# Ninety-six stores of a weight conversion, begun by GpSimd instead of SyncE

## The chip, the cores and the metric

The kernel runs on one core of a Trainium2 chip. The time is device microseconds of one execution, from the first to the last instruction on that core and what lies around them. The engines of the core have queues of their own and work through them in order: TensorE (PE in the profile, with its weight loads as PEld), VectorE (DVE), ScalarE (ACT), GpSimd (POOL) and SyncE (SP), which here only begins transfers. Sixteen DMA engines carry the transfers of all of them.

## The reference

Attention with the heads mixed before and after the softmax, followed by a two-layer feed-forward net. All of it is float32.

```python
# q, k, v: (8, 12, 448, 64); w_pre, w_post: (12, 12)
scores = (1 / 8) * q @ k^T                          # per batch and head
scores = einsum('bhij,hg->bgij', scores, w_pre)     # mix the heads
attn = exp(scores - max) ; attn /= sum(attn) + 1e-9
attn = einsum('bhij,hg->bgij', attn, w_post)        # mix the heads again
x = (attn @ v), heads side by side: (3584, 768)
h = x @ w_in                                        # (768, 2048)
out = (h - tanh(h)) @ w_out                         # (2048, 768)
```

## The kernel before, in words

The program has two stages. The first, up to about 850 us, is attention; the second is the feed-forward net. The second stage multiplies in a split form (a high and a low part of each number) and takes seven products where eight are usual, so it needs the weights of `w_in` and `w_out` as high and low parts, and sums of their quarters in the same form. These are made once, during the first stage, by the class `Convert` and its generator `narrow_quad`, and written to tensors in the chip's DRAM: `wi` and `wo` hold the split weights, `ss` and `ts` the split sums. The second stage loads them from there.

**Attention.** 448 query rows of each of 8 batches are cut into blocks of 120, 120, 120 and 88 rows, and these into groups of at most ten rows times twelve heads. Two groups make a *place*; there are 180 places (`NPL`), and the loop over `p` writes one place after another. In place `p`:

- SP begins the gathers of a later place: `gather` (L907) copies the scores of ten rows and twelve heads from the tile `s` into one of six tiles `t`, 210 KB each, for place `p + 2`.
- SP then begins up to six other transfers that were put into two lists, `queue` (loads of q, k, v, stores of `x`) and `slow` (all transfers of the conversion); `send`, L766, is the line that begins each.
- PE mixes the heads of place `p` (`premix`, L918, tile `ps_p`). DVE takes the row maximum (L927), ACT the exponential (L929) with its sum.
- For place `p - 1`, `norm` makes the weights of the second mix: DVE adds 1e-9 (L938), takes the reciprocal `zs` (L939), and POOL multiplies `w_post` by it (L940), which gives `wr`, the *mix weights*.
- PE does what the plan put into the place: scores of a later block (L874), the product with `v` (L999), transposes (L814, L840).
- PE does the second mix of place `p - 1` (`mix`, L957): 32 small products that read `wr`. ACT copies their result out at the start of the next place (L967).

**The conversion.** There are 48 *quads* of weights, 24 of `w_in` and 24 of `w_out`. Each goes through seven steps, one in each place, from the fifth place on; a new one starts at most every third place. `conv.place()` stands at the head of a place, ahead of all that is listed above, so the work of the conversion stands ahead of that place's `wr` in the queue of POOL. POOL's part is: step 2, a scaling (L84, 1.49 us); step 4, two products (L96, L97); step 5, three or four sums (L116 to L119, or L128 to L130); step 6, the low part of the weights (L103) and the high part of the sums (L105); step 7, the low part of the sums (L108). Behind step 6 the tile `co` is written to `wi` or `wo`, behind step 7 the tile `ct` to `ss` or `ts`, 512 KB each time. These 96 stores are entered into `slow`, between the 96 loads of the conversion, and SP begins them in the same place, behind the gathers.

**What sets the order.** Every engine's queue is kept in the order in which the program is written (`in_order`). An instruction that waits holds up all that stands behind it on its engine.

Of the kernel before, what the change touches and what calls it, by code (L numbers as in the profile page):

```python
# [21 lines left out]
def raw(ap):  # L22

    return ap.bitcast(F32)
# [10 lines left out]
class Convert:  # L35


    def __init__(self, nc, pool, dma, items, places):
        self.nc, self.pool, self.dma = nc, pool, dma
        self.todo, self.loads, self.active = list(items), [], []  # L40
        self.rate, self.due = len(self.todo) / places, 1.0

    def load(self):
# [6 lines left out]
    def place(self):  # L50
        for x in list(self.active):
            next(x[0], None)
            x[1] += 1
            if x[1] == 7:
                self.active.remove(x)
        self.due = min(self.due + self.rate, 1.3)
        if self.due >= 1.0 and len(self.active) < 2 and not [x for x in self.active if x[1] < 4] and self.loads and self.loads[0][1]():
            r, _, to = self.loads.pop(0)
            self.active.append([narrow_quad(self.nc, self.pool, self.dma, r, *to), 1])
            next(self.active[-1][0])  # L60
            self.due -= 1.0
        if self.todo and len(self.loads) < 2 and len(self.loads) + len([x for x in self.active if x[1] < 5]) < 3:
            self.load()

    def rest(self, between):
        while self.todo or self.loads or self.active:
            self.due = 1.0
            self.place()
            between()


def narrow_quad(nc, pool, dma, r, dst, sums, sums_dst):

    p = r.shape[0]
    hi, lo = r[:, :, :, 1], r[:, :, :, 0]
    u, w = hi, lo


    lim = 122879.9921875
    m = pool.tile([p, 4, 128], F32, name="cm", tag="cm", bufs=2)  # L80
    nc.vector.tensor_scalar(m, hi.bitcast(F32), lim, -lim, op0=ALU.min, op1=ALU.max)
    nc.vector.tensor_scalar(w, lo, 8, None, op0=ALU.logical_shift_right)
    yield
    nc.gpsimd.tensor_scalar(m, m, 2.0**-112, None, op0=ALU.mult)  # L84
    nc.scalar.mul(w.bitcast(F32), w, 2.0**-44)
    yield
    o = pool.tile([p, 4, 2, 128], F32R, name="co", tag="co", bufs=2)
    oh, ol = o[:, :, 0], o[:, :, 1]
    s = ol.bitcast(I32)
    nc.vector.tensor_scalar(s, hi, -(2**31), None, op0=ALU.bitwise_and)  # L90
    nc.vector.scalar_tensor_tensor(
        out=u, in0=m.bitcast(I32), scalar=3, in1=s, op0=ALU.logical_shift_left, op1=ALU.bitwise_or
    )
    nc.vector.tensor_scalar(s, u, -(2**23), None, op0=ALU.bitwise_and)
    yield
    nc.gpsimd.tensor_tensor(out=m, in0=w.bitcast(F32), in1=s.bitcast(F32), op=ALU.mult)  # L96
    nc.gpsimd.tensor_tensor(out=m, in0=m, in1=u.bitcast(F32), op=ALU.add)  # L97
    yield
    t = pool.tile([p, 4, 2, 128], F32, name="ct", tag="ct", bufs=2)
    nc.scalar.copy(oh, m)  # L100
    done = sums(nc, m, t[:, :, 1])
    yield
    nc.gpsimd.tensor_sub(ol, m, raw(oh))  # L103
    done()
    nc.gpsimd.tensor_copy(t[:, :, 0].bitcast(F32R), t[:, :, 1])  # L105
    dma(dst, raw(o).rearrange("p x t n -> p x (t n)"))
    yield
    nc.gpsimd.tensor_sub(t[:, :, 1].bitcast(F32R), t[:, :, 1], t[:, :, 0])  # L108
    dma(sums_dst, t.rearrange("p s t n -> p s (t n)"))


def sums_in(nc, m, t):
# [38 lines left out]
def kernel_body(  # L151
# [11 lines left out]
    nc = tc.nc  # L163
# [206 lines left out]
    class Results:  # L370
# [145 lines left out]
        def store(self, b, t, h, c):  # L516
            to = out[b * TB + t * TT : b * TB + (t + 1) * TT, h * N2 : (h + 1) * N2]
            eng = nc.gpsimd if self.n_gr < len(self.grs) else nc.sync
            eng.dma_start(to, c.rearrange("p c n -> p (c n)"))
# [216 lines left out]
    with ExitStack() as st:  # L736
# [196 lines left out]
        def norm(p):  # L933
            zs = te[p][1]
            wr = gp.tile([P, 2, D], F32, name="wr", tag="wr", bufs=2)[:, :, :HP]
            for r in range(2):

                nc.vector.tensor_scalar_add(zs[:, 1, r : r + 1], zs[:, 0, r : r + 1], 1e-9)  # L938
            nc.vector.reciprocal(zs[:, 2], zs[:, 1])  # L939
            nc.gpsimd.tensor_mul(  # L940
                wr, wpost[:, :HP].unsqueeze(1).to_broadcast([P, 2, HP]), zs[:, 2].unsqueeze(2).to_broadcast([P, 2, HP])
            )
            te[p].append(wr)
# [137 lines left out]
        for w in range(2):  # L1081
            for at in AT[w]:
                x = repeat[:, w, at : at + HP].rearrange("p (i h) -> p i h", i=GH)
# [7 lines left out]
        for w in range(2):  # L1091
            for a in range(2):
                if w == 0:
                    x = both[:, w, a].rearrange("p (i g) -> p i g", i=GH)
                    of, step = ps_w[:, w, :].unsqueeze(1).to_broadcast([P, GH, H]), [[H, GH], [0, H]]
                else:
                    x = both[:, w, a].rearrange("p (g i) -> p g i", i=GH)
# [44 lines left out]
        conv = Convert(nc, cv, partial(dma, to=slow), quads, NPL - 24)  # L1142
# [22 lines left out]
        at_s, p, kind = {}, 0, None  # L1165
        window = {i: (lo, hi) for lo, hi, k, i, _ in sorted(halved, reverse=True) if k == "s"}
        while halved:
            ready = sorted((x for x in halved if x[0] <= p), key=lambda x: (x[1], x[3:]))
            if ready:
                x = ready[0]  # L1170
# [3 lines left out]
                if x[2] == kind and other and x[1] > p + 1:  # L1174
                    x = other[0]
# [80 lines left out]
        for p in range(NPL + 3):  # L1256
# [14 lines left out]
                ps = premix(p)  # L1271
            if 1 <= p < NPL + 1:
                norm(p - 1)
            if p == NPL:
                for f in x0[1:]:
                    f()
# [118 lines left out]
```

## Time and profile before

| | |
|---|---|
| runs | 1704.64, 1707.81 and 1708.6 us; median 1707.81 us |
| profiled execution | 1703.0 us, of which the span from first to last instruction is 1701.3 us |
| granted clock of TensorE | 0.994 over the span |
| busy | PE 1660.1 us, DVE 1231.3 us, ACT 1091.1 us, POOL 585.5 us |
| first `wr` of POOL, last `wr` | 30.2 us, 842.4 us: 180 places, 4.5 us each |
| stores of the conversion | 96 of 512 KB, the first begun at 72.1 us, the last at 781.5 us |

In the rows below, a line such as `L957 PE MATMUL ps_o<-wr,e` names the line of the kernel, the engine, the operation and the tiles (written `out<-in`). A bracket at the end of a row of the timeline gives the time for which the engine had stood idle, and what ended it. SPq stands for SP's queue, in which the begin of a transfer takes the time shown. Rows that count waits give the sum in us, the number of waits, and the longest.

### The profile page before, as it was taken

The page shows a single profiled execution, that of the slowest core. Times are in us where ns is not written, and L with a number is a line of the kernel's source. Part 1 is how long each engine was busy: PE and PEld are TensorE (multiplying, and loading weights), DVE is VectorE, ACT ScalarE, POOL GpSimd, SP SyncE. Part 2 cuts the span into 40 slices and gives each one's busy share as a digit, 9 for nine tenths or more (in the row PEclk, how much of TensorE's full clock was granted, in tenths as well). Part 3 has the DMA queues.
Part 4 walks back from the last instruction along what each step waited for, and adds up shares of the span by engine and source line. Part 5 has one row for each costly group of instructions (what it writes and reads, how often), then busy time and mean ns, then how long its engine had stood idle before and what let it go on. Part 6 is the DMA issues. An engine that isn't in the chain of part 4 may idle for free.

```text
span 1701.3 us, 41215 instructions
## 1 busy us (share of the span) xinstructions
PE 1660.1 (98%) x16068; PEld 1379.8 (81%) x16068; DVE 1231.3 (72%) x2119; ACT 1091.1 (64%) x1920; POOL 585.5 (34%) x798
## 2 busy tenths in 40 slices
PE   8999999999999899999999999999999999999999
PEld 6777777777777677677788888888888888989999
DVE  5777777878777777675497899868778867778432
ACT  5777777777777677676586777556667456666331
POOL 1466667666666666662100111101001101011100
PEclk9999999999999999999999999999999999999999
DMA  8879889898987979856589899989999989988993
GB/s 183 218 228 257 255 246 276 247 270 259 256 253 231 269 234 257 254 182 208 190 269 340 273 331 318 346 295 335 318 334 362 368 272 327 326 311 327 404 413 132
DMA packets 322290, 475.09 MB, mean 279 GB/s; under 512 B 105264, under 2 KB 255280, under 8 KB 322096
## 3 DMA queue, kind: packets, MB, share of 16 engines
q1 hardware_dynamic: 305660, 414.34, 75.5%
q0 software_dynamic: 16128, 57.68, 8.7%
q8 instruction: 128, 2.10, 0.5%
q14 instruction: 66, 0.54, 0.1%
q10 hardware_dynamic: 308, 0.43, 0.1%
HBM read 274.73 MB, written 120.59 MB: 232 GB/s over the span
## 4 chain that ended last, share of the span: by engine, by line
PE 72%; DMA 7%; DVE 7%; ACT 4%; issue 4%; POOL 4%; SPq 1%; POOLq 0%; ACTq 0%; DVEq 0%
PE ps_o L957 11%; PE ps_h L291 8%; PE ps_h L292 7%; PE ps_h L294 7%; PE ps_m L999 6%; PE ps_p L918 6%; PE y L534 6%; PE y L532 6%; PE y L533 6%; PE ps_q L874 4%; DMA t<-s 2%; DMA gl<-gs 2%; ACT e L929 1%; DVE mx L927 1%; PE y L504 1%
## 5 line engine op out<-in xcount | busy, mean ns | idle before, releaser
L957 PEld LDWEIGHTS ps_o<-wr,e 60*112 60x112 f32 (+1 forms) x5760 | 303.3, 175 | 46.1 <-POOL wr L940 31.9
L957 PE MATMUL ps_o<-wr,e 60*112 60x60 f32 (+1 forms) x5760 | 314.5, 259 | 16.1 <-POOL wr L940 14.6
L929 ACT ACTIVATE e<-ps_p,mx 128x448 f32<-128x448 f32 x360 | 224.8, 631 | 117.2 <-DVE mx L927 82.8
L927 DVE TENSOR_REDUCE mx<-ps_p 128x1 f32<-128x448 f32 x360 | 206.5, 615 | 109.1 <-PE ps_p L918 108.5
L967 ACT COPY at<-ps_o 112x960 f32<-112x960 f32 x156 | 154.3, 989 | 103.4 <-PE ps_o L957 102.9
L918 PE MATMUL ps_p<-t,wpre 60*64 60x448 f32 (+1 forms) x1440 | 182.4, 570 | 6.7 <-DMA t<-s 6.6
L999 PEld LDWEIGHTS ps_m<-at,vr 112*64 112x64 f32 x3072 | 147.6, 137 | 23.0 <-issue 7.7
L999 PE MATMUL ps_m<-at,vr 112*64 112x120 f32 (+1 forms) x3072 | 161.4, 262 | 1.1 <-DMA vr<-in_v_dram 0.9
L532 PE MATMUL y<-w,gh 128*128 128x384 f32 x448 | 151.2, 338 | 2.1 <-DMA w<-wo 1.6
L940 POOL TENSOR_TENSOR wr<-wpost,zs 128x120 f32<-128x120 f32 x180 | 70.0, 389 | 237.6 <-DVE zs L939 199.0
L533 PE MATMUL y<-w,gh 128*128 128x384 f32 x448 | 150.5, 336 | 0.0
L534 PE MATMUL y<-w,gl 128*128 128x384 f32 x424 | 143.4, 338 | 3.0 <-DVE gl L450 3.0
L874 PEld LDWEIGHTS ps_q<-kk,qh 64*120 64x120 f32 (+1 forms) x768 | 59.1, 174 | 82.0 <-issue 45.1
L874 PE MATMUL ps_q<-kk,qh 64*120 64x448 f32 (+1 forms) x768 | 121.8, 394 | 0.9 <-ACT kk L825 0.4
L879 DVE COPY s<-ps_q 120x448 f32<-120x448 f32 (+1 forms) x192 | 112.2, 614 | 9.8 <-PE ps_q L874 8.0
L669 POOL DMA_DIRECT2D gs<-gb x24 | 17.2, 717 | 291.6 <-DVE gb L668 291.6
L307 ACT ACTIVATE u<-h 128x1024 f32<-128x1024 f32 x56 | 59.5, 1063 | 74.4 <-DVE h L716 70.5
L879 ACT COPY s<-ps_q 120x448 f32<-120x448 f32 (+1 forms) x192 | 94.9, 538 | 7.1 <-PE ps_q L874 6.7
L647 POOL DMA_DIRECT2D gs<-ga x24 | 17.2, 716 | 230.0 <-DVE ga L330 222.9
L532 PEld LDWEIGHTS y<-w,gh 128*128 128x128 f32 x448 | 84.2, 188 | 7.2 <-issue 3.5
L533 PEld LDWEIGHTS y<-w,gh 128*128 128x128 f32 x448 | 84.1, 188 | 3.4
L534 PEld LDWEIGHTS y<-w,gl 128*128 128x128 f32 x424 | 79.6, 188 | 4.6 <-DVE gl L450 4.6
(372 smaller groups left out, 3971.3 us busy)
## 6 DMA issues: line engine op xcount, KB each, us to landing
t<-s SPq DMA_DIRECT2D x342, 210.0 KB
wa<-ss SPq DMA_DIRECT2D x96, 384.0 KB
w<-wo SPq DMA_DIRECT2D x43, 768.0 KB
gl<-gs SPq DMA_DIRECT2D x62, 512.0 KB
wa<-wi SPq DMA_DIRECT2D x72, 384.0 KB
w<-ts SPq DMA_DIRECT2D x35, 768.0 KB
gs<-gs POOLq DMA_DIRECT2D x24, 768.0 KB, 9.2
cr<-in_moe_w_in_dram SPq DMA_DIRECT2D x48, 256.0 KB
```

The source lines that it names most:

```text
L291: nc.tensor.matmul(ph, w[:, c, 0], xh, start=start and c == 0, stop=False, skip_group_check=True)
L532: nc.tensor.matmul(y, gh[:, tok], wh, start=first, stop=False, skip_group_check=True)
L533: nc.tensor.matmul(y, gh[:, tok], wl, start=False, stop=False, skip_group_check=True)
L534: nc.tensor.matmul(y, gl[:, tok], wh, start=False, stop=last, skip_group_check=True)
L874: nc.tensor.matmul(ps[:n, :S], qx[a, hp, :], kx[a, hp % 2], start=(x == 0), stop=(x == 2))
L879: eng(sts[i][:n, 2 * hp + j, :], ps[:n, :S])
L918: nc.tensor.matmul(pss[r][halves[j], :], wpre[k, :], ts[j][k, :], start=True, stop=True)
L927: nc.vector.tensor_reduce(out=mx, in_=ps, axis=AX.X, op=ALU.max, negate=True)
L929: nc.scalar.activation(e, ps, AF.Exp, bias=mx, scale=1.0, accum_out=zs[:, 0, r : r + 1])
L957: nc.tensor.matmul(ps[:CP, j, c * GP : (c + 1) * GP].rearrange("p (h i) -> p h i", i=GI)[:, :, r * GH : (r + 1) * GH], e[k, c * CP : (c + ...
L967: nc.scalar.copy(ats[i0][:, :, :, at : at + 2 * GI].rearrange("p c h (j i) -> p j (c h) i", j=2), ps[:CP, :, : NC * GP].rearrange("p j (x ...
L999: nc.tensor.matmul(pv[j * D : (j + 1) * D, r, :n], vt[:, j, c, :], ats[i][:, c, 2 * hp + j, :n], start=(c == 0), stop=(c == NC - 1),)
```

## The change

`narrow_quad` is handed a function that only notes a finished store in a list, `done`. A new method `stores` begins all noted stores from GpSimd's queue and clears the list. The place loop calls it right behind `norm(p - 1)`, so behind that place's `wr`. The loads of the conversion stay in `slow` and with SP.

```diff
@@ class Convert
-        self.todo, self.loads, self.active = list(items), [], []
+        self.todo, self.loads, self.active, self.done = list(items), [], [], []
@@ def place
-            self.active.append([narrow_quad(self.nc, self.pool, self.dma, r, *to), 1])
+            self.active.append([narrow_quad(self.nc, self.pool, lambda *x: self.done.append(x), r, *to), 1])
@@
+    def stores(self):
+        for x in self.done:
+            self.nc.gpsimd.dma_start(*x)
+        self.done.clear()
+
     def rest(self, between):
         while self.todo or self.loads or self.active:
             self.due = 1.0
             self.place()
+            self.stores()
             between()
@@ def narrow_quad
-    dma(dst, raw(o).rearrange("p x t n -> p x (t n)"))
+    store(dst, raw(o).rearrange("p x t n -> p x (t n)"))
     yield
     nc.gpsimd.tensor_sub(t[:, :, 1].bitcast(F32R), t[:, :, 1], t[:, :, 0])
-    dma(sums_dst, t.rearrange("p s t n -> p s (t n)"))
+    store(sums_dst, t.rearrange("p s t n -> p s (t n)"))
@@ the loop over places
             if 1 <= p < NPL + 1:
                 norm(p - 1)
+            conv.stores()
             if p == NPL:
```

The instructions of PE, DVE and ACT stand as before. Two queues change; in the changed kernel all line numbers from L60 on are six or seven higher (L940 is now L946, L108 is L114).

POOL's queue in two places in a row early in the conversion, before. `wr` is the mix weights; `L103` and `L105` are step 6 of a quad, `L108` is its step 7, and `L96`, `L97` are step 4 of the next quad.

```order
L103 TENSOR_TENSOR co<-cm,co 128x4x128
L105 CAST ct<-ct 128x4x128
L940 TENSOR_TENSOR wr<-wpost,zs 128x2x60
L108 TENSOR_TENSOR ct<-ct 128x4x128
L96 TENSOR_TENSOR cm<-cr,co 128x512
L97 TENSOR_TENSOR cm<-cm,cr 128x512
L940 TENSOR_TENSOR wr<-wpost,zs 128x2x60
L116 TENSOR_TENSOR ct<-cm 128x128
```

The same places in the changed kernel:

```order
L109 TENSOR_TENSOR co<-cm,co 128x4x128
L111 CAST ct<-ct 128x4x128
L946 TENSOR_TENSOR wr<-wpost,zs 128x2x60
L67 DMA wi_65<-co 512x1x256
L114 TENSOR_TENSOR ct<-ct 128x4x128
L102 TENSOR_TENSOR cm<-cr,co 128x512
L103 TENSOR_TENSOR cm<-cm,cr 128x512
L946 TENSOR_TENSOR wr<-wpost,zs 128x2x60
L67 DMA ss_77<-ct 512x1x256
L122 TENSOR_TENSOR ct<-cm 128x128
```

The store of `co` now stands behind the `wr` of its place and ahead of `L114`, and with it ahead of all that POOL does before the next `wr`; the store of `ct` stands likewise one place later.

SP's queue over the same stretch, before:

```order
L907 DMA t<-s 120x1x448 x2
L766 DMA wi_65<-co 512x1x256
L907 DMA t<-s 120x1x448 x2
L766 DMA ss_77<-ct 512x1x256
L907 DMA t<-s 120x1x448 x2
L766 DMA cr<-in_moe_w_in_dram 128x2x256 x2
```

and in the changed kernel:

```order
L913 DMA t<-s 120x1x448 x6
L772 DMA cr<-in_moe_w_in_dram 128x2x256 x2
```

The two stores are gone from between the gathers; the loads of the next quad follow the third pair of gathers as before.

More of the change, by code (lines that the diff above doesn't have):

```diff
@@ L68, in rest, with narrow_quad @@
             self.place()
+            self.stores()
             between()
-def narrow_quad(nc, pool, dma, r, dst, sums, sums_dst):
+def narrow_quad(nc, pool, store, r, dst, sums, sums_dst):
     p = r.shape[0]
```

## The prediction

> **What bounds the kernel now.** I began with the head of the page (busy us, share of the span, instructions).
>
> ```profile
> PE 1660.1 (98%) x16068; PEld 1379.8 (81%) x16068; DVE 1231.3 (72%) x2119; ACT 1091.1 (64%) x1920; POOL 585.5 (34%) x798
> ```
>
> Then the table of busy time by stretches (columns: length of the stretch, then PE, PEld, DVE, ACT and POOL busy with their counts, the granted clock, the DMA share, GB/s):
>
> ```profile
> 200.00:300.00 100.00, 97.95 (x1456) 76.06 (x1456) 73.88 (x189) 72.41 (x165) 67.54 (x90) 1.00 0.88 262
> 500.00:600.00 100.00, 94.19 (x1358) 71.10 (x1354) 74.01 (x182) 70.52 (x166) 65.73 (x80) 0.98 0.85 253
> ```
>
> PE is the bound, in the attention stage too: it is busy for 94 to 98 us of each 100. POOL's 34% over the span hides that it is busy for two thirds of the time while the conversion runs. The change touches nothing outside this stage, so the question is what PE waits for there. The waits of PE between 60 and 850 us (sum, number, longest):
>
> ```profile
> PE ps_o L957 <- POOL wr L940: 14.4, 16, 1.7
> PE ps_p L918 <- DMA t<-s: 5.0, 7, 1.0
> PE ps_m L999 <- DMA vr<-in_v_dram: 0.9, 1, 0.9
> ```
>
> That is nearly everything: 14.4 us for the mix weights of POOL, 5.0 us for gathers of SP. The change takes work out of the second chain and puts it into the first.
>
> **What leaves SP.** Ninety-six stores leave its queue. They could delay a gather in two ways: by waiting for POOL at the head of the queue, and by the time of their own issue. The waits in SP's queue:
>
> ```profile
> SPq L907 <- PE ps_q L874: 135.0, 71, 5.0
> SPq L766 <- POOL co L103: 14.4, 9, 4.4
> SPq L766 <- POOL ct L108: 13.1, 11, 4.7
> ```
>
> At 71 places SP stood at a gather with time to spare and waited for PE to free its tile, so a store ahead of it cost nothing there. What remains are the gathers PE did wait for. Three of the seven stand behind a store whose issue took long:
>
> ```profile
> 471.35 5.46 SPq L766 DMA_DIRECT2D wo<-co  x1
> 476.99 1.96 SPq L907 DMA_DIRECT2D t<-s  x2
> 483.23 0.98 PE L918 MATMUL ps_p<-t,wpre 60*64 60x448 f32 x8 [0.72 <-DMA t<-s]
> 570.14 6.12 SPq L766 DMA_DIRECT2D ts<-ct  x1
> 576.36 1.74 SPq L907 DMA_DIRECT2D t<-s  x2
> 572.26 0.98 PE L918 MATMUL ps_p<-t,wpre 60*64 60x448 f32 x8 [0.67 <-DMA t<-s]
> 577.18 0.98 PE L918 MATMUL ps_p<-t,wpre 60*64 60x448 f32 x8 [0.99 <-DMA t<-s]
> 158.61 5.63 SPq L766 DMA_DIRECT2D cr<-in_moe_w_in_dram  x1
> ```
>
> They come to 0.72 + 0.67 + 0.99 = 2.4 us. A load of `cr` shows the same long issue (5.63 us at 158.61), so it may simply strike another transfer next time. The gain lies between 0 and 5.0 us; I take the 2.4 us. The bytes are the same whoever begins them, so I count nothing for the DMA engines.
>
> **What POOL gets.** Ninety-six transfers to begin. In this stage POOL begins none now; the nearest rows are those it begins later (columns: busy sum and mean ns of one, then the idle time before them), beside its own rows that matter here:
>
> ```profile
> L940 POOL TENSOR_TENSOR wr<-wpost,zs 128x120 f32<-128x120 f32 x180 | 70.0, 389 | 237.6 <-DVE zs L939 199.0 <-DMA t<-s 9.4 <-PE ps_p L918 8.0
> L519 POOL DMA_DIRECT2D out_dram<-c x48 | 25.9, 546 | 137.1 <-DVE c L551 73.9 <-ACT c L542 56.0 <-ACT c L510 5.2
> L669 POOL DMA_DIRECT2D gs<-gb x24 | 17.2, 717 | 291.6 <-DVE gb L668 291.6
> L670 POOL DMA_DIRECT2D gs<-gs x24 | 18.2, 758 | 0.0
> ```
>
> By the shapes in the code, L519 writes 128 separate runs of DRAM, L669 writes 256 and L670 384. A store of the conversion writes 512 runs of 1 KB. A line through the first and the last, 546 + (758 - 546) / 256 x 384, gives 0.86 us, which I take. The lower bound is nothing: no row shows whether POOL could compute while it begins a transfer. What speaks against it is that a second transfer behind a first started only at the first one's end:
>
> ```profile
> 956.56 0.73 POOL L669 DMA_DIRECT2D gs<-gb  x1 [9.43 <-DVE gb L668]
> 957.29 0.75 POOL L670 DMA_DIRECT2D gs<-gs  x1
> ```
>
> The upper bound is 1.43 us: 512 runs as two transfers of 256, 2 x 717 ns.
>
> In sum that is 96 x 0.86 = 83 us of POOL, but only what arrives late at PE counts. The store itself waits for nothing: its tile was finished ahead of the `wr` that it stands behind. Behind it, though, stand the next steps of the conversion and then the next `wr`, for which PE waits. Where POOL stood idle before one of these instructions, the idle time swallows the store; in all, POOL stood idle for 237.6 us before its `wr`, most of it waiting for DVE's `zs`. Where it did not, the store passes on in full. One such place:
>
> ```profile
> 209.87 0.39 POOL L940 TENSOR_TENSOR wr<-wpost,zs 128x120 f32<-128x120 f32 x1 [3.54 <-DVE zs L939]
> 210.21 1.26 POOL L108 TENSOR_TENSOR ct<-ct 128x512 fp32r<-128x512 f32 x1
> 211.44 1.48 POOL L96 TENSOR_TENSOR cm<-cr,co 128x512 f32<-128x512 f32 x1
> 213.00 1.37 POOL L97 TENSOR_TENSOR cm<-cm,cr 128x512 f32<-128x512 f32 x1
> 214.33 0.38 POOL L940 TENSOR_TENSOR wr<-wpost,zs 128x120 f32<-128x120 f32 x1
> 213.36 0.17 DVE L939 RECIPROCAL zs<-zs 128x2 f32<-128x2 f32 x1
> 214.76 1.79 PE L957 MATMUL ps_o<-wr,e 60*112 60x60 f32 x32 [0.36 <-POOL wr L940]
> ```
>
> `zs` was done at 213.53, POOL reached its `wr` at 214.33, and PE had already waited 0.36 us when the mix began at 214.76. The store of `co` will stand between the first two rows: the second `wr` and the mix come 0.8 us later, and that is PE's own time.
>
> I followed POOL's rows in this way from the first of the 180 `wr` (at 30.2 us) to the last (842.4 us): after each `wr` behind an L105 or an L108 the delay grows by the store, each idle time of POOL takes away from it, and what is left at a `wr` counts against the margin between the end of that `wr` and the start of its mix on PE. (Where PE loses time, the delay shrinks by as much, since PE's later work moves too.) With 0.86 us, 54 `wr` come late, 19 of them later than PE's margin, and PE loses 8.5 us, or 9.9 us if the margin is measured to the first weight load of the mix instead. I take 9. With 0.54 us it is 4 to 5 us, with 0 nothing, with 1.43 us 27 to 30 us: the loss grows faster than the price, because idle time runs out.
>
> Does DVE suffer? The conversion's own DVE rows already collide with POOL's:
>
> ```profile
> L82 DVE TENSOR_SCALAR cr<-cr x48: 409/420/1524, 51.9 to 753.3; 128x512 int32<-128x512 int32 x48
> L94 DVE TENSOR_SCALAR co<-cr x48: 426/427/1377, 60.4 to 762.7; 128x512 int32<-128x512 int32 x48
> ```
>
> The same 512 elements take 0.42 us, or up to 1.52 us while POOL works. A store behind `wr` starts while DVE does the maximum of the next place (L927, two rows of 0.6 us, read from PSUM), so 0.86 us of store is mostly over before the next L82. I count nothing; if the cover goes, that is the second rival below.
>
> **The sum.** 1703.0 us of the profiled execution - 2.4 + 9 = 1709.6 us, which is 6.6 us more, or 0.4%. The runs shown have their median at 1707.8 us, 4.8 us above the profiled one; on that scale the forecast is 1707.8 + 6.6 = 1714 us. A difference under 0.3%, about 5 us, can't be told from none in this kernel, so the forecast stands only just outside.
>
> **The rivals.** *The stores disappear in POOL's idle time.* If one costs 0.5 us or less on POOL, PE loses at most 4.5 us and gets 2.4 back: 1706 to 1710 us. For it: L519, whose 546 ns would be the price if the number of runs did not matter, and the 237.6 us of idle time. Against it: L669 and L670 cost 30 to 40% more than L519.
>
> *A store holds POOL much longer.* At 1.43 us the sum is 27 to 30 - 2.4, so 1733 to 1735 us. The mechanism: beginning a transfer from POOL and a DVE row that works from SBUF hold each other up, as L82 shows with 1.1 us of delay against POOL's compute rows. A store that begins late, because its `wr` waited for the conversion, meets L81 or L82. It decides from about 1.2 us per store on. Against it: no such stretched transfer stands among the rows above, where the mean of L670 is 758 ns. The Trainium skill has this as a rule (SBUF — State Buffer, section "SBUF: two separate sides"): while DVE runs an operation in a mode that takes both port pairs, GpSimd can't write the descriptors of its transfer, and a transfer of some 620 ns took about 3100 ns; its advice is to begin such transfers from ACT or SP. As an estimate by that figure for every store, which no run here shows, the loss would be several times that of 1.43 us. The trace agrees that 0.42 us rows of DVE stretch beside POOL, to 1.52 us.
>
> *Faster.* All gather waits of 5.0 us go, with the 0.9 us for `vr`, because SP never stands at a store again, while POOL begins a store without holding up its own computing. Then 1707.8 - 5.9 = 1702 us. It decides only if a store costs POOL under about 0.1 us; above that the first loss eats what 5.9 us leave over the 5 us bound. For it: nothing in the rows excludes that computing goes on beside a transfer's begin. Against it: four of the seven waits stand behind no store.
>
> **How the numbers follow.** The forecast, a store of 0.7 to 1.1 us and a net loss of about 4 to 14 us, gets 0.47: 0.37 of it beyond 5 us, 0.10 within. Hidden stores get 0.26, nearly all of it no change (0.24), 0.02 faster. Long stores get 0.17, all slower. The faster case gets 0.10, 0.08 of it beyond the bound, 0.02 within. So 0.10 faster, 0.36 the same, 0.54 slower. The range runs from 1704 us (a store at no cost, 2.4 to 4 us gained) to 1733 us (1.43 us per store); the forecast's own range is 1710 to 1722 us.
>
> **What would show it.** On the page after: 96 new rows of POOL, transfers `wi`, `wo`, `ss`, `ts`, at some 0.86 us each, and POOL busy for about 83 us more. The wait of PE at L957 (then L963) for `wr` should rise from 14.4 to about 23 us, the one for gathers fall from 5.0 to about 2.6 us. In the place of the example the mix should wait about 1.1 us, not 0.36. The second stage should keep its length. The prediction is wrong if POOL's rows behind a store start before the store's row ends, if a store takes under 0.5 or over 1.2 us, or if PE's wait for gathers rises, which would mean that stores from a second queue take bandwidth at worse moments.

## The result

The change makes the kernel slower by 46 us: 1753.66 us in the median (1751.44 to 1755.23, 4 runs) against 1707.37 us before (1704.64 to 1708.6, 4 runs). The ratio is 1.0263 with a 95% interval of 1.0241 to 1.0286, which is 41 to 49 us. The prediction had the sign right and the size wrong: 1714 us, at most 1733.

The profiled execution took 1752.7 us, 49.7 us more than the one before, and this is what has to be found. The head of its page (busy us, share of the span, instructions):

```profile
PE 1687.5 (96%) x16068; PEld 1391.6 (79%) x16068; DVE 1279.0 (73%) x2119; ACT 1094.0 (62%) x1920; POOL 665.3 (38%) x894
```

There are 96 more instructions on POOL, as announced, and 80 us more of its time. But DVE, whose instructions are the same 2119, is busy for 48 us more (1231.3 before), and PE for 27 us more with the same matmuls. The table of busy time by stretches, first of the kernel before, then of the changed one (columns: length, then PE, PEld, DVE, ACT and POOL busy with their counts, granted clock, DMA share, GB/s):

```profile
0.00:900.00 900.00, 872.93 (x12086) 671.92 (x12087) 649.84 (x1567) 633.31 (x1397) 505.04 (x674) 0.99 0.81 241
950.00:1703.00 753.00, 738.73 (x3761) 668.02 (x3759) 544.54 (x521) 423.51 (x485) 77.61 (x119) 1.00 0.89 323
```

```profile
0.00:900.00 900.00, 850.25 (x11783) 643.01 (x11784) 651.66 (x1530) 596.04 (x1355) 582.32 (x766) 0.96 0.76 225
1000.00:1753.00 753.00, 739.04 (x3769) 667.69 (x3767) 546.62 (x522) 425.20 (x487) 77.89 (x119) 1.00 0.89 323
```

The last 753 us of both are alike, so the loss lies in the attention stage. In the first 900 us PE stood idle for 22.7 us more (872.93 - 850.25), and what it did it did at a lower clock, 0.96 in the place of 0.99. Summed over 180 windows of 5 us (window times 1 - clock), the time lost to the clock was 8.5 us before and 32.5 us after. Twenty-three us of idle PE and 24 us of slow clock are the two halves of the loss in this pair of executions. The granted clock of all runs gives the clock a little less: over the span it was 0.979 to 0.981 in the four runs of the change and 0.984 to 0.999 in 48 runs of the kernel before, which is 34 us lost in the mean against 15.

The waits of PE between 60 and 900 us (sum, number, longest):

```profile
PE ps_o L963 <- POOL wr L946: 35.0, 39, 2.4
PE ps_m L1005 <- DMA vr<-in_v_dram: 4.1, 3, 3.5
PE ps_p L924 <- ACT co L106: 1.5, 1, 1.5
PE ps_p L924 <- DMA t<-s: 1.0, 2, 0.7
```

The mix weights cost 20.6 us more than before (14.4), `vr` 3.2 us more (0.9), ACT's copy to `co` 1.5 us that no row showed before, and the gathers 4.0 us less (5.0). That makes 21.3 us, and with the clock's 24.0 it is 45 of the 49.7. The groups of POOL that hold the new rows (sum and mean ns of one, then the idle time before them):

```profile
L67 POOL DMA_DIRECT2D wo<-co x24 | 20.5, 856 | 0.2 <-POOL wr L946 0.2
L67 POOL DMA_DIRECT2D wi<-co x24 | 18.4, 766 | 2.6 <-POOL wr L946 0.9
L67 POOL DMA_DIRECT2D ss<-ct x24 | 17.5, 729 | 2.6 <-issue 1.5 <-POOL wr L946 0.8 <-DMA t<-s 0.2
L67 POOL DMA_DIRECT2D ts<-ct x24 | 17.5, 727 | 2.7 <-issue 1.8 <-POOL wr L946 0.6 <-DMA qr<-in_q_dram 0.2
```

The price of a store is 0.77 us in the mean, less than the 0.86 us that the prediction took. So the mistake isn't in the price. It shows in the groups of DVE, in the two clamping rows with which a quad begins; before, and after:

```profile
L82 DVE TENSOR_SCALAR cr<-cr 128x512 int32<-128x512 int32 x48 | 37.9, 790 | 0.0
L81 DVE TENSOR_SCALAR cm<-cr 128x512 f32<-128x512 f32 x48 | 37.4, 779 | 2.3 <-DMA cr<-in_moe_w_in_dram 2.3
```

```profile
L87 DVE TENSOR_SCALAR cm<-cr 128x512 f32<-128x512 f32 x48 | 57.8, 1204 | 0.9 <-DMA cr<-in_moe_w_in_dram 0.9
L88 DVE TENSOR_SCALAR cr<-cr 128x512 int32<-128x512 int32 x48 | 56.5, 1178 | 0.0
```

The same two operations on the same 512 elements take 0.8 us more per quad, 39 us over the 48 quads. That is most of DVE's 48 us.

**One place, row by row.** This is the prediction's example. DVE before, then POOL, DVE and PE of the changed kernel (start, length, and in brackets the idle time before a row and what ended it):

```profile
211.22 0.54 DVE L81 TENSOR_SCALAR cm<-cr 128x512 f32<-128x512 f32 x1
211.68 1.52 DVE L82 TENSOR_SCALAR cr<-cr 128x512 int32<-128x512 int32 x1
```

```profile
217.34 0.39 POOL L946 TENSOR_TENSOR wr<-wpost,zs 128x120 f32<-128x120 f32 x1 [2.83 <-DVE zs L945]
217.88 0.76 POOL L67 DMA_DIRECT2D wi<-co  x1
218.62 1.32 POOL L114 TENSOR_TENSOR ct<-ct 128x512 fp32r<-128x512 f32 x1
219.85 1.35 POOL L102 TENSOR_TENSOR cm<-cr,co 128x512 f32<-128x512 f32 x1
221.28 1.36 POOL L103 TENSOR_TENSOR cm<-cm,cr 128x512 f32<-128x512 f32 x1
223.39 0.39 POOL L946 TENSOR_TENSOR wr<-wpost,zs 128x120 f32<-128x120 f32 x1 [0.75 <-DVE zs L945]
218.69 2.80 DVE L87 TENSOR_SCALAR cm<-cr 128x512 f32<-128x512 f32 x1
221.41 1.51 DVE L88 TENSOR_SCALAR cr<-cr 128x512 int32<-128x512 int32 x1
223.08 0.17 DVE L945 RECIPROCAL zs<-zs 128x2 f32<-128x2 f32 x1
223.83 3.25 PE L963 MATMUL ps_o<-wr,e 60*112 60x60 f32 x32 [1.94 <-POOL wr L946]
```

Before, the two `wr` started 4.46 us apart (209.87 and 214.33, rows in the prediction). Now it is 6.05 us: a store of 0.76 us has put the second one off by 1.59 us, and PE waits for 1.94 us where it waited for 0.36. The extra 0.8 us comes through DVE. Its first clamping row met POOL's `L108` before: POOL's row ended at 211.47, the clamp 0.29 us later, at 211.76, in the opening between `L108` and `L96`. The second clamp then lay through `L96` (end 212.92) and ended 0.28 us behind it. Now the first clamp meets `L114` (end 219.94) but isn't let through: it ends at 221.49, 0.29 us behind `L102`. The second one lies through `L103` and ends 0.28 us behind that, at 222.92. `zs` stands behind both on DVE, and POOL, done with its own work at 222.64, waits 0.75 us for it. The Trainium skill has the rule that fits (SBUF — State Buffer, section "SBUF: two separate sides"): a DVE operation in a two-port mode and a GpSimd operation take a shared pair of ports for a whole instruction, and the other one waits. The 0.28 us behind a POOL row agree with it. Its warning about such transfers, which the prediction quoted, is the other way round. None of the 96 store rows was stretched, but this hardly tests the warning: only five of them ran beside one of the conversion's rows on DVE, and most beside rows that read PSUM. The longest stands in this group (shortest, median and longest in ns, then the first and last start):

```profile
L67 POOL DMA_DIRECT2D wi<-co x24: 730/768/915, 75.1 to 440.0; - x24
```

I classed all 48 first clamps by the POOL rows that they overlap. A clamp is held by a row if it lasts to that row's end. Before, six clamps were still running when `L108` ended, and none of them lasted to the end of `L96`: all were let through in the opening. After, 14 were still running when `L114` ended, and all 14 lasted to the end of `L102`. The second clamp was free 31 times before and 8 times after.

The same can be read from PE's waits for `wr`, sorted by whether POOL had stood idle for `zs` ahead of that `wr`, and whether clamps stood ahead of that `zs` on DVE. Behind such a `zs` PE waited for 2.4 us before and 17.5 us after; behind another late `zs` for 6.2 and 8.7 us; behind POOL's own rows for 5.8 and 8.8 us. So 15.1 of the 20.6 us came through a `zs` that stands behind clamps.

What the stall then costs can be read from the same table by stretches, for 2 us each:

```profile
222.00:224.00 2.00, 0.17 (x2) 0.17 (x4) 1.97 (x6) 0.12 (x1) 1.10 (x3) 0.95 0.02 8
224.00:226.00 2.00, 2.00 (x24) 2.00 (x24) 1.64 (x6) 2.00 (x6) 1.92 (x4) 0.50 0.40 141
226.00:228.00 2.00, 2.00 (x20) 1.20 (x18) 0.00 (x0) 0.95 (x2) 2.00 (x4) 0.50 0.51 180
228.00:230.00 2.00, 2.00 (x14) 1.09 (x6) 1.16 (x2) 1.62 (x4) 1.65 (x3) 0.50 0.82 238
230.00:232.00 2.00, 2.00 (x33) 1.91 (x34) 0.70 (x2) 1.63 (x6) 0.52 (x1) 0.84 0.82 294
```

A stall of 1.94 us is followed by 6.8 us at half the clock. The mix takes 3.25 us instead of 1.78, and the stall has cost 3.4 us more than itself. From 60 to 880 us there are 9 such stretches after and 4 before. Each of the nine began during a stall of 1.4 to 3.5 us, or within 2 us of its end.

### The profile page after: what moved, and what is told of

It reads as the page before. It is cut to its first block, busy times and chain, and to the rows that moved or that the text cites. A ratio compares the mean times of both kernels' runs of the same rounds, so it can differ in the third digit from the quotient of the medians.

```text
span 1751.0 us, 41176 instructions
## 1 busy us (share of the span) xinstructions
PE 1687.5 (96%) x16068; PEld 1391.6 (79%) x16068; DVE 1279.0 (73%) x2119; ACT 1094.0 (62%) x1920; POOL 665.3 (38%) x894
## 4 chain that ended last, share of the span: by engine, by line
PE 68%; DVE 14%; DMA 7%; ACT 5%; issue 3%; POOL 3%; SPq 0%; DVEq 0%; ACTq 0%; POOLq 0%
PE ps_o L963 10%; PE ps_h L297 7%; PE ps_h L298 7%; PE ps_h L300 7%; PE ps_p L924 6%; PE y L540 6%; PE y L538 6%; PE y L539 6%; PE ps_m L1005 6%; PE ps_q L880 4%; ACT e L935 2%; DVE mx L933 2%; DVE cm L87 2%; DVE cr L88 2%; DMA vr<-in_v_dram 1%
## 5 line engine op out<-in xcount | busy, mean ns | idle before, releaser
L963 PEld LDWEIGHTS ps_o<-wr,e 60*112 60x112 f32 (+1 forms) x5760 | 310.6, 179 | 75.3 <-POOL wr L946 63.1
L963 PE MATMUL ps_o<-wr,e 60*112 60x60 f32 (+1 forms) x5760 | 325.5, 264 | 36.8 <-POOL wr L946 35.2
L924 PE MATMUL ps_p<-t,wpre 60*64 60x448 f32 (+1 forms) x1440 | 186.7, 585 | 5.2 <-DMA t<-s 2.6
L946 POOL TENSOR_TENSOR wr<-wpost,zs 128x120 f32<-128x120 f32 x180 | 69.9, 388 | 214.9 <-DVE zs L945 176.0
L880 PE MATMUL ps_q<-kk,qh 64*120 64x448 f32 (+1 forms) x768 | 126.5, 404 | 1.3 <-DVE kk L832 0.5
```

The lines of the kernel that those rows point to most:

```text
L880: nc.tensor.matmul(ps[:n, :S], qx[a, hp, :], kx[a, hp % 2], start=(x == 0), stop=(x == 2))
L924: nc.tensor.matmul(pss[r][halves[j], :], wpre[k, :], ts[j][k, :], start=True, stop=True)
L963: nc.tensor.matmul(ps[:CP, j, c * GP : (c + 1) * GP].rearrange("p (h i) -> p h i", i=GI)[:, :, r * GH : (r + 1) * GH], e[k, c * CP : (c + ...
```

## The experiments

Differences in us are the ratio's distance from 1 times 1708, with its 95% interval. "Clock" is the time lost to a lower clock in the first 900 us, worked out as above, "wait" PE's wait for `wr`, "clamp" the mean of the first clamping row in ns; all three are from one profiled execution and scatter with it (two kernels of the same time below have 8.5 and 15.3 us of clock). The changed kernel stands on that scale at +45 us (41 to 49), clock 32.5, wait 35.0, clamp 1204; the kernel before at clock 8.5, wait 14.4, clamp 779. Where a share of the clock matters, the mean over all runs of a kernel is better, taken over the whole span: 15 us lost before, 34 in the change, 14 with the filler, 22 with the stores begun by ScalarE, 24 with both.

The expectations set theories against each other. Theory A: what counts is time on POOL, which reaches PE through the held clamps and the late `zs`. Theory B: it is the beginning of transfers on POOL, or the second queue of transfers beside SP's. Theory C, made later, is that POOL's rows lose the opening between them behind the begin of a transfer.

| kernel | median us (range) | difference us | clock | wait | clamp |
|---|---|---|---|---|---|
| filler of 0.79 us on POOL | 1721.2 (1718.3–1722.9) | +13 (9–18) | 15.3 | 25.5 | 720 |
| stores begun by ScalarE | 1718.3 (1715.8–1722.6) | +11 (7–14) | 27.3 | 13.7 | 789 |
| both of these | 1731.9 (1727.8–1739.2) | +23 (17–29) | 20.5 | 26.7 | 714 |
| only stores of `co` on POOL | 1746.3 (1734.3–1752.4) | +37 (29–45) | 34.4 | 29.5 | 1203 |
| only stores of `ct` on POOL | 1731.3 (1727.2–1737.4) | +22 (17–28) | 32.3 | 19.9 | 827 |
| change, clamps late | 1734.2 (1730.7–1734.9) | +28 (23–33) | 20.5 | 25.2 | 811 |
| before, clamps late | 1710.3 (1702.5–1715.2) | +1 (-4–6) | 15.3 | 13.6 | 649 |
| change, both stores later | 1810.4 (1806.8–1815.0) | +105 (99–112) | 66.5 | 65.5 | 820 |
| change, two rows behind a store | 1757.9 (1747.3–1773.4) | +55 (41–68) | 32.4 | 41.4 | 798 |
| filler of 1.15 us on POOL | 1739.8 (1736.8–1751.0) | +32 (25–38) | 23.9 | 35.7 | 748 |
| filler of 0.79 us, clamps late | 1720.0 (1712.4–1724.4) | +9 (5–13) | 17.0 | 23.3 | 844 |
| small transfers begun on POOL | 1731.6 (1727.1–1738.9) | +23 (17–28) | 22.2 | 29.4 | 1042 |

### Time on POOL alone, and a second queue alone

The first kernel is the one before, with a memset on POOL where the change has a store.

```diff
@@ kernel before, class Convert
+    def fill(self):
+        for _ in range(self.n):
+            self.nc.gpsimd.memset(self.pool.tile([128, 832], F32, name="fill", tag="fill"), 0.0)
+        self.n = 0
@@ the loop over places, behind norm(p - 1)
+            conv.fill()
```

> The stores stay with SP; behind the mix weights, where the changed kernel begins a store, GpSimd only fills a scratch tile of 128x832 numbers, about 0.75 us. Theory A (GpSimd's time: the two products of step 4 come later, VectorE's two clamping rows L81 and L82 are held until these end, zs comes late, TensorE waits and its clock drops): 35 to 50 us slower than before, L82's mean at 1.1 to 1.3 us where it was 0.79, granted clock near 0.98. Theory B (it is the beginning of transfers on GpSimd, or their second queue beside the gathers): within 8 us of before, L82 near 0.8 us. The prediction's own sum (GpSimd's lateness alone): 7 to 9 us slower.

Its groups on POOL and DVE, and then PE's wait:

```profile
L72 POOL MEMSET fill<- 128x832 f32 x96 | 76.1, 792 | 0.0
L91 DVE TENSOR_SCALAR cm<-cr 128x512 f32<-128x512 f32 x48 | 34.5, 720 | 2.0 <-DMA cr<-in_moe_w_in_dram 2.0
L92 DVE TENSOR_SCALAR cr<-cr 128x512 int32<-128x512 int32 x48 | 53.7, 1118 | 0.0
```

```profile
PE ps_o L967 <- POOL wr L950: 25.5, 31, 2.0
```

The filler takes as long on POOL as a store, and costs 13 us, not 45. PE's wait rises to 25.5 us, near the prediction's 23: for a row that only takes time, the replay was about right. The second clamp is held as in the change (1118 ns), the first is not (720).

The second kernel is the changed one with the stores begun by ScalarE, in the same place of the program.

```diff
@@ changed kernel, stores
-            self.nc.gpsimd.dma_start(*x)
+            self.nc.scalar.dma_start(*x)
```

> The 96 stores are begun by ScalarE at the same place of the program, so they leave SP and take a second queue, but GpSimd gets nothing. Theory A: within 8 us of before on either side (up to 5 us gained at gathers, a few lost on ScalarE, which spends some 0.6 us per store), L82 near 0.8 us. Theory B in the form of the second queue: 20 to 45 us slower, with longer waits for gathers.

The waits of PE:

```profile
PE ps_o L963 <- POOL wr L946: 13.7, 14, 1.7
PE ps_m L1005 <- DMA vr<-in_v_dram: 4.0, 3, 2.3
PE ps_p L924 <- ACT co L106: 1.6, 1, 1.6
```

The wait for `wr` is that of the kernel before, and yet 11 us are lost. The waits for `vr` and for ACT's `co` stand at 4.0 and 1.6 us as in the change, so these belong to the stores having left SP, not to POOL. The profiled execution, at the upper end of this kernel's runs, lies 19.5 us over the one before, and 18.8 us of that is clock (27.3 - 8.5): short waits, many of them followed by a slow stretch. By all runs it is about 8 of the 11 us (22 lost against 14 in the eight runs of the kernel before made beside it). In the Trainium skill (DMA: Bandwidth & Descriptors, section "Issuing engines are not separate DMA queues") beginning transfers on several engines only saves the sequencer's time for the begin. The runs say that moving them can still cost. SP, rid of the stores' waits, reaches its loads at other times; that this is the reason was not tried.

Both together: ScalarE begins the stores, and POOL has a filler of 0.79 us for each.

```diff
@@ changed kernel, stores
-            self.nc.gpsimd.dma_start(*x)
+            self.nc.scalar.dma_start(*x)
+            self.nc.gpsimd.memset(self.pool.tile([128, 832], F32, name="fill", tag="fill"), 0.0)
```

> The changed kernel, with each store begun by ScalarE instead of GpSimd, and a memset of 0.79 us on POOL where the store stood. POOL gets the same time as in the change, and the stores leave SP's queue, but POOL begins no transfer. Nothing of the computation is left out. Theory A (time on POOL and a second queue, each with its own price: the filler alone cost 13 us, ScalarE's stores alone 10 us): the two add up, 18 to 28 us over the kernel before. Rival C (a transfer begun on POOL leaves its following rows without an opening for DVE): the same 18 to 28 us here, and the 20 us that the change costs beyond that belong to the begin on POOL itself; the clamping rows of DVE take about 0.72 and 1.12 us as with the filler, not 1.20 and 1.18. Rival D (the two prices multiply, since a late mix and a late load strike each other): 40 us or more, without longer clamping rows; then nothing is left for the begin on POOL.

The clamping rows:

```profile
L88 DVE TENSOR_SCALAR cm<-cr 128x512 f32<-128x512 f32 x48 | 34.3, 714 | 1.7 <-DMA cr<-in_moe_w_in_dram 1.7
L89 DVE TENSOR_SCALAR cr<-cr 128x512 int32<-128x512 int32 x48 | 56.1, 1168 | 0.0
```

13 and 11 us add up to 23. POOL has about the same time to spend as in the change, and the same transfers are off SP; what differs is that ScalarE begins them and not POOL. That is worth 22 us (15 to 29), half of the loss, and of the clamping rows it is the first that differs (714 ns, not 1204); the second is as long as in the change (1168 and 1178).

### One kind of store at a time

The stores of `co` on POOL and those of `ct` on SP, and the reverse:

```diff
@@ changed kernel: only co on POOL
-    store(sums_dst, t.rearrange("p s t n -> p s (t n)"))
+    dma(sums_dst, t.rearrange("p s t n -> p s (t n)"))
@@ changed kernel: only ct on POOL
-    store(dst, raw(o).rearrange("p x t n -> p x (t n)"))
+    dma(dst, raw(o).rearrange("p x t n -> p x (t n)"))
```

> Only the 48 stores of co are begun by GpSimd, ahead of the place with the three long rows (step 7 of one quad, step 4 of the next); those of ct stay with SP. Theory A: this half carries most of the loss, 25 to 45 us slower than before. Theory B: half of the loss, about 24 us. The prediction's own sum: about 5 us.

> Only the 48 stores of ct are begun by GpSimd, ahead of the place with the sums (step 5); those of co stay with SP. Theory A: 0 to 12 us slower than before, since the clamping rows stand in the other place and only GpSimd's own lateness counts. Theory B: half of the loss, about 24 us.

The first clamping row with `co` on POOL, the same with `ct` on POOL, and the gather waits of the latter:

```profile
L87 DVE TENSOR_SCALAR cm<-cr 128x512 f32<-128x512 f32 x48 | 57.8, 1203 | 1.4 <-DMA cr<-in_moe_w_in_dram 1.4
```

```profile
L87 DVE TENSOR_SCALAR cm<-cr 128x512 f32<-128x512 f32 x48 | 39.7, 827 | 0.8 <-DMA cr<-in_moe_w_in_dram 0.8
```

```profile
PE ps_p L924 <- DMA t<-s: 10.1, 8, 2.2
```

The store of `co` stands right ahead of `L114` and `L102`, which the first clamp meets, and this half alone has the 1203 ns, and a loss of 37 us. Without it the first clamp is at 827 ns and never held by both rows (with it, 14 times). The 22 us of the `ct` stores are more than I expected by time on POOL (0 to 12). The profiled execution lies 34.4 us over the one before; 23.8 us of that is clock, the gather waits rise by 5.1 us (10.1 against 5.0) and the wait for `wr` by 5.5. Why the gathers wait more when half of the stores stay with SP is open. The two halves lose 59 us together and the whole change 45, so neither figure is a share of the whole.

### The clamping rows moved away

The two clamps are written behind the row maxima of their place, so behind `zs`, which they then can't hold up. The same was done to the kernel before, and later to that with the filler.

```diff
@@ class Convert
-            next(self.active[-1][0])
+            self.new = self.active[-1][0]
@@
+    def begin(self):
+        if self.new:
+            next(self.new)
+            self.new = None
@@ the loop over places
             if p < NPL:
                 expo(p, ps)
+            conv.begin()
```

> The changed kernel, with VectorE's two clamping rows of a new quad (step 1) written behind the row maxima of the place, not ahead of zs. Theory A (the clamping rows, held until GpSimd's products end, make zs and the mix weights late): TensorE's wait for the mix weights falls from 35 us to under 18, time 0 to 15 us above before. Theory B (the transfers themselves): still 30 us or more above before.

> The kernel before, stores with SP, with the same move of the two clamping rows. Theory A: the 8.9 us that TensorE waited behind a late zs shrink, so 3 to 12 us faster than before. If the clamping rows then hold up the copies of the scores instead, no difference within 5 us. Theory B says nothing here.

> The kernel before with the memset of 0.79 us on POOL, and with DVE's two clamping rows written behind the row maxima and zs of their place, so that they can't hold up zs. Nothing of the computation is left out. The filler alone cost 13 us (PE's wait for wr 25.5 us), the move alone nothing (2 us). Theory A in its full form (the filler's loss goes through the held clamping rows): 0 to 7 us, PE's wait for wr 14 to 20 us. Rival (the filler's loss is POOL's own lateness, as the prediction's replay had it): 10 to 18 us as without the move, PE's wait 23 us or more, nearly all of it behind POOL's own rows.

PE's wait for `wr` in the changed kernel, in the one before and in the one with the filler, each with late clamps:

```profile
PE ps_o L970 <- POOL wr L953: 25.2, 31, 1.8
```

```profile
PE ps_o L964 <- POOL wr L947: 13.6, 14, 1.7
```

```profile
PE ps_o L974 <- POOL wr L957: 23.3, 29, 1.7
```

The move does nothing to the kernel before, where 3 to 12 us were expected, and gives back 17 us of the change's 45, and 10 of 35 us of waiting. With the filler it gives back little: 13 becomes 9 us, intervals overlapping. There, part of what waited behind a late `zs` now waits behind POOL's own rows. Sorted by whether POOL stood idle for `zs` ahead of the `wr` or was still at work, the filler's 25.5 us were 12.7 and 12.8; with late clamps they are 7.9 and 15.4. In the change 26.2 us of the 35.0 stood behind a late `zs`; with late clamps 9.4 of 25.2. So my theory in its full form, that all loss goes through the clamps, is wrong for plain time on POOL, where the rival was nearer, and fits what the begin of a transfer adds. The changed kernel with late clamps (28 us) is about what filler and second queue give with late clamps (9 + 11 = 20 us, 12 to 27 by the intervals): little special is left.

### What about the begin closes the opening

To test theory C, the stores were kept with SP, and POOL began a transfer of 32 KB in 128 runs at each of the same places, from a tile of zeros to a tensor that nobody reads.

```diff
@@ changed kernel, class Convert
+    def both(self, *x):
+        self.dma(*x)
+        self.done.append(x)
@@ stores
-        for x in self.done:
-            self.nc.gpsimd.dma_start(*x)
+        for _ in self.done:
+            self.nc.gpsimd.dma_start(self.far[self.n], self.near)
+            self.n += 1
```

> The kernel before (all 96 stores stay with SP), and at each place where the change begins a store, POOL begins a small transfer instead: 128 runs of 256 B, 32 KB, from a tile of zeros to a tensor that nobody reads. Nothing of the computation is left out. By the row of 546 ns for 128 runs I expect 0.4 to 0.6 us on POOL each. Theory A alone (only POOL's time counts; 0.79 us cost 13 us): 3 to 12 us, the first clamping row of DVE at 0.72 to 0.80 us and not held by the rows L114 and L102 together. Theory C (any begin of a transfer on POOL takes away the opening between the rows behind it): 18 to 35 us, the first clamping row at 1.0 us or more, held by both rows some 12 times. If C holds only for long transfers (512 runs), the result is that of A, and then the length of a begin, not the begin, decides.

The groups with these begins and with the first clamp, and then PE's wait:

```profile
L72 POOL DMA_DIRECT2D far<-near x96 | 57.4, 598 | 4.2 <-issue 1.9
L93 DVE TENSOR_SCALAR cm<-cr 128x512 f32<-128x512 f32 x48 | 50.0, 1042 | 1.3 <-DMA cr<-in_moe_w_in_dram 1.3
```

```profile
PE ps_o L969 <- POOL wr L952: 29.4, 37, 2.2
```

A begin of 0.60 us costs 23 us, with no store moved and a sixteenth of the bytes, where a filler of 0.79 us costs 13. The first clamp is at 1042 ns. Fourteen clamps were still running when the first of the two POOL rows ended, and all 14 were held by the second too. With the filler there were twelve such clamps, with the longer filler below eight, and none was held by the second row.

How far does each put POOL off? From the start of `wr` to the start of `L102` (median over the places where POOL did not wait in between) it is 1.58 us before, 2.29 with the small transfer, 2.32 with the filler and 2.45 in the change. Where the sums stand behind, the next row comes 0.61 us later with the small transfer, 0.74 with the filler and 0.69 in the change. So the small transfer takes no more of POOL's time than the filler and costs 9 us more (2 to 16). It is the begin on POOL that does it, not its time, its 512 runs or its bytes.

Next, the change with two tiny rows on POOL behind each store, the second reading what the first wrote, and the control for their time, the kernel before with a longer filler:

```diff
@@ changed kernel, stores
             self.nc.gpsimd.dma_start(*x)
+            one = self.pool.tile([128, 8], F32, name="one", tag="one", bufs=2)
+            two = self.pool.tile([128, 8], F32, name="two", tag="two", bufs=2)
+            self.nc.gpsimd.memset(one, 0.0)
+            self.nc.gpsimd.tensor_copy(two, one)
@@ kernel with the filler
-            self.nc.gpsimd.memset(self.pool.tile([128, 832], F32, name="fill", tag="fill"), 0.0)
+            self.nc.gpsimd.memset(self.pool.tile([128, 1260], F32, name="fill", tag="fill"), 0.0)
```

> The changed kernel, with a fill of eight columns and a dependent copy of them on GpSimd behind each store, so that GpSimd's next rows start only when all of it is done with the store. Theory C (after a store the rows of GpSimd run into each other without the opening in which VectorE gets in between L108 and L96, so the first clamping row is held by both): the rows held by both fall from 14 to under 4, its mean from 1.2 to 0.8 us, and the time falls to 15 to 30 us above before although GpSimd has some 25 us more to do. Theory A alone: GpSimd's time is what counts, so slower than the changed kernel by 5 to 15 us.

> The kernel before with a memset of about 1.17 us on POOL (128x1260 numbers) where the change puts a store; the stores stay with SP. Nothing of the computation is left out. With 0.79 us it was 13 us. Theory A (idle time of POOL runs out, so the loss grows faster than the price): 25 to 40 us, PE's wait for wr 33 to 45 us. Rival (each us on POOL costs the same): 19 us. If it is 46 us or more, the change is explained by a store that is in effect longer than its row shows, with no need for the rows behind it; if it is below 25 us, that is excluded, since no store row is as long as 1.17 us in the mean.

The groups of the first kernel, and then the filler of the second:

```profile
L71 POOL COPY two<-one 128x8 f32<-128x8 f32 x96 | 20.3, 212 | 6.1
L70 POOL MEMSET one<- 128x8 f32 x96 | 17.4, 181 | 0.0
L91 DVE TENSOR_SCALAR cm<-cr 128x512 f32<-128x512 f32 x48 | 38.3, 798 | 1.2 <-DMA cr<-in_moe_w_in_dram 1.2
```

```profile
L72 POOL MEMSET fill<- 128x1260 f32 x96 | 110.2, 1148 | 0.0
```

With two rows between, the opening is back: the first clamp is at 798 ns, and none of the eight clamps that were still running when `L114` ended was held by `L102` too. The time is another matter: theory C expected 15 to 30 us above before. But store and rows take 0.77 + 0.39 = 1.16 us, and a filler of 1.15 us already costs 32 us, and with the 11 us of the second queue 43. The 55 us (41 to 68) of this kernel can't be told from that, nor from the change's 45, so its time speaks neither for theory C nor against it. The two fillers also show how the price grows: 45% more time on POOL, 2.4 times the loss.

### Both stores later

Both stores of a quad were begun together, behind the `wr` of the place after step 7.

```diff
@@ changed kernel, stores
+        if len(self.done) < 2 or not self.held:
+            self.held = len(self.done) > 1
+            return
+        self.held = False
         for x in self.done:
             self.nc.gpsimd.dma_start(*x)
```

> The changed kernel, with both stores of a quad begun together behind the mix weights of the place after step 7, ahead of the place with step 6, in which GpSimd has the least to do. Theory A: the products of step 4 are not delayed, so the second clamping row (L88 in the changed kernel) is held about as often as before (mean near 0.8 us) and the time is 3 to 20 us above before. Theory B: the same transfers on the same queue, so as slow as the changed kernel, 40 to 50 us above.

The group of DVE that stood still longest, and then PE's wait:

```profile
L101 DVE TENSOR_SCALAR co<-cr 128x512 int32<-128x512 int32 x48 | 26.4, 551 | 66.0 <-DMA wi<-co 36.1 <-DMA wo<-co 29.8
```

```profile
PE ps_o L968 <- POOL wr L951: 65.5, 34, 7.5
```

Both expected times were missed, and the time says nothing about the theories. With two tiles `co`, a store begun later frees its tile later, and DVE waited 66.0 us for that, with `zs` behind it. The clamps, for which the run was made, were little held (820 ns). No kernel here was faster than the one before.

## Why the prediction was wrong, step by step

- **What bounds the kernel: right.** PE in the attention stage, and `wr` as what it waits for. The second stage kept its length.
- **What leaves SP: the gain came, but not by that reckoning; the rest was missed.** Gathers went from 5.0 to 1.0 us where 2.6 were expected. Of the three waits that made up the 2.4 us, two (0.67 and 0.99) were for gathers begun at 565.65 and 568.53 us, ahead of the long store at 570.14; only the 0.72 us stood behind a long store. Why the others went as well is open, so that the gain came is luck. "I count nothing for the DMA engines" failed in its neighbourhood: `vr` rose from 0.9 to 4.1 us, and the second queue by itself costs 11 us.
- **The price of a store: right.** 0.77 us, not 0.86, and below the 1.2 us from which the second rival was to decide. The rows behind a store started at its end, to within 0.03 us (218.64 and 218.62 in the example). None of the signs listed as making the prediction wrong appeared: no price out of bounds, no overlap, no longer gather wait. It was wrong all the same.
- **The replay: the step that failed.** "Each idle time of POOL takes away from it" left every `zs` where it stood and moved only POOL. But where clamps stand ahead of a `zs`, as for 55.9 of the 199.0 us that POOL waited for `zs`, a held clamp ends 0.28 us behind a row of POOL, so the `zs` moves with POOL's rows and can become what the next `wr` waits for. In the example the replay's 0.8 us was 1.59. Over the stage PE's wait for `wr` rose by 20.6 us where 9 were expected, 15.1 of it through such a `zs` and 3.0 behind POOL's own rows, the part that the replay followed.
- **"Does DVE suffer? … I count nothing": the same step from the other side.** The prediction had the row that shows it, `L82` at 0.42 to 1.52 us, but asked only whether the store itself would cover a clamp. Not the store but the rows behind it do, and behind a begun transfer two in a row. Compared at about equal time on POOL, with the stores off SP in both, that is 22 of 45 us (15 to 29).
- **The clock: not in the sum.** Each lost us was counted once. Stalls of 1.4 to 3.5 us drew stretches at half the clock, and this took 24 us of the 49.7 in the profiled pair, and about 20 of 46 by the granted clock of all runs.
- **The rivals.** The longer hold gave a time nearer the truth (1733 to 1735 us), but by a price that did not come. Hidden stores and a gain were both out.

The accounting is then 13 us for time on POOL, 11 us for the second queue, and 22 us for the begin on POOL. As an estimate from the mean clock of all runs, the clock's share in these is nothing, 8 us and 10 us. Why a begin closes the opening is open. In the example `L102` starts 0.09 us ahead of `L114`'s end, and in the mean of 36 such pairs 0.08 us, against 0.04 before, behind a filler and behind the two tiny rows, and 0.05 behind a small transfer. That would fit parts of GpSimd out of step with each other, as the Trainium skill describes (GPSIMD Engine Reference, section "Instruction dispatch": the next instruction isn't held back until all cores have done the last one). But POOL's ends are rough in these records, and this is argued, not shown.

## What to carry to other kernels

Before you let an engine's idle time swallow new work, ask what ends that idle time; if the releaser itself runs behind a row of this engine, here through DVE rows that POOL's rows hold, the idle time moves along, and new work can lengthen the wait by more than itself. A filler of the same length, the same instruction with a trivial load, and the same transfers from another engine separate time, kind and queue in three runs. On an engine that bounds the kernel, price a stall together with the clock that it loses.

## What the runs showed of the hardware

- A stall of 1.94 us of PE was followed by 6.8 us at half the granted clock. It isn't every time: 6 us earlier in the changed kernel a mix behind a stall of 1.51 us ran at its full 1.78 us. What tells the two apart is how they fall on a grid. All stretches at half clock in this trace begin on one grid of 3.41 us and last one, two or three of its windows. The stall of 1.94 us lay within one window, in which PE was busy for 1.50 of 3.41 us; the one of 1.51 us fell across two, with 2.71 and 2.60 us. From 60 to 880 us the nine falls of the clock came behind windows in which PE was busy for 33 to 59%; of the windows without a fall, one had 57% and all others 62% or more. The Trainium skill (TensorE: Matmul & The Clock Gate, section "What's actually happening") names an idle window of about 3.4 us for this; here a window that was 41% idle was enough.

```profile
217.78 1.78 PE L963 MATMUL ps_o<-wr,e 60*112 60x60 f32 x32 [1.51 <-POOL wr L946]
```

- Beginning 128 runs of 256 B took POOL 0.60 us and 512 runs of 1 KB 0.73 to 0.86 us: four times the runs at 1.2 to 1.4 times the price.
- A DVE clamp that had to wait for POOL ended 0.28 to 0.30 us behind the end of a row of POOL (24 first clamps before, 35 in the change). If it met the first of two rows of POOL behind the begin of a transfer, it was held through both (14 of 14 behind a store, 14 of 14 behind a small transfer); behind a memset of 0.79 or 1.15 us it was held through the first alone (12 of 12 and 8 of 8).
- The begin of the same store took ScalarE's queue 0.52 us and POOL 0.73 to 0.86.
